# Loading q and k in runs of eight rows, sorting them on VectorE and turning all of them by DMA

## The chip, the core and the metric

The kernel runs on one core of one Trainium2 chip. The core has four compute engines with one instruction queue each: TensorE (PE in the profile) multiplies matrices and writes to PSUM, VectorE (DVE) and ScalarE (ACT) work element by element, and GpSimd (POOL) does simple element work and issues the DMAs that convert float32 to bfloat16. SyncE (SP) computes nothing; its queue issues the remaining DMAs, the transposing ones among them. Each engine takes its own instructions strictly in order, and an instruction that waits for a semaphore holds back everything behind it on the same engine.

The metric is the time of one execution on the device in microseconds. Before the change it is 306.56 us (median of 3 runs, 305.95 to 306.98).

## The reference

Sliding-window causal attention is followed by a two-matrix network with an x·cos(x) gate. Shapes: q, k and v are (8 batches, 8 heads, 576 positions, 64), `w_in` is 512 x 2048, `w_out` 2048 x 512, and the output 4608 x 512 in float32.

```python
window = 64
scores = (q @ k.transpose(0, 1, 3, 2)) / sqrt(64)
rel = pos[:, None] - pos[None, :]
scores = where((rel >= 0) & (rel < window), scores, -1e9)
attn = softmax(scores)
x = (attn @ v).transpose(0, 2, 1, 3).reshape(4608, 512)
h = x @ w_in
out = (h * cos(h)) @ w_out
```

## The kernel before

**Tiles of tokens.** The 4608 rows of x are nine tiles of 512 tokens. Tile 0 is handled by steps written out by hand (the string `FIRST`). Tiles 1 to 8 go through the loop over `mt`; one turn of it is called a stage here. A stage has two halves. In the first, TensorE makes sixteen products `h_ps` (L458, four matmuls each), ScalarE takes a sine of each (L597), and VectorE multiplies the two into `gT` (L600); these sixteen multiplications are called gates 0 to 15. In the second half TensorE makes four products `out_ps` (L611), each of which sums over all sixteen slices of `gT` in order. The sixteen `h_ps` take turns in five PSUM banks, so TensorE can be at most five products ahead of the gates.

**Attention.** In stage b-1 the scores of batch b are computed in two bursts (`burst_scores`, matmuls at L289), one just after the first half of the stage and one in the second half. They go in nine groups per batch: VectorE masks and takes the maximum (`g_max`, L326), ScalarE takes exponentials (`g_exp`, L338), GpSimd normalizes into `w` (`g_norm`, L355), and SP turns `w` into `wT` by a transposing DMA (`g_trans`, L374). At the end of the stage `values` (L390) multiplies `wT` with v, and `put_x` copies the result to `xT`, the input of the next stage. Of batch b's nine groups the next stage's tile needs only the first ones: four at stage 1's end (besides two that go through TensorE), five at stage 2's, four at stage 3's and 4's, two at stage 5's.

**q and k.** The scores need q and k with the head dimension on the partitions, so both must be turned. For batches 0 and 1 this is done on TensorE. For batches 2 to 7, `load_chunk` (L166) loads each of q and k in six chunks of 96 positions, all eight heads at once: rows of 64 numbers, issued by GpSimd, converted to bfloat16 on the way. Chunks of k are turned by DMA (`turn_k`, L239, six per batch). Of q, `TURNED` gives the number of chunks that DMA turns (`turn_q`, L227): none for batches 2 and 3, two for 4, 5 and 6, and six for 7. The remaining chunks are turned by TensorE (`transposed`, L203, into the PSUM tile `tq_ps`) and copied to SBUF by VectorE (`put_q`, a COPY at L121).

**The order.** Nothing is scheduled automatically. `at(time, function, ...)` puts steps on a list, and `pump(time)` issues those that are due; 32 units of that time make a stage, gate `ff` is followed by `pump(base + ff)`, and the second half covers units 16 to 32. The order of the steps in this list is the order on every engine's queue, SP's and GpSimd's among them. `t0 - T` in the code is the start of stage b-2, `t0` that of stage b-1.

Of the kernel before, what the change touches and what calls it, by code (L numbers as in the profile page):

```python
# [10 lines left out]
def _safe_warn(msg, *a, **kw):  # L11
# [13 lines left out]
NC, NP = 6, 96  # L25
# [5 lines left out]
RC = 9  # L31
# [8 lines left out]
TURNED = {4: 2, 5: 2, 6: 2, 7: 6}  # L40
# [26 lines left out]
def kernel(  # L67
# [28 lines left out]
    qsets = [const.tile([128, PAIRS, S], BF16, name=f"qT{i}") for i in range(2)]  # L96
    vtiles = [const.tile([128, NU - 1, d_model], BF16, name=f"v{i}") for i in range(2)]
# [44 lines left out]
    def rows_tile(name):  # L142
        return ld.tile([128, NC * H * D], BF16, tag=name, name=name)

    def load_heads(name, b, p0=0, n=PAIRS):
        if (name, b) not in st:
            st[name, b] = rows_tile(name)[:, 0:PAIRS * RC * D].rearrange("p (a x) -> p a x", a=PAIRS)
        src = {"q": q, "k": k}[name][b, 2 * p0:2 * p0 + 2 * n]
        nc.gpsimd.dma_start(out=st[name, b][:, p0:p0 + n],  # L149
                            in_=src.rearrange("(a h) (p c) d -> (h p) a (c d)", h=2, c=RC))  # L150
# [6 lines left out]
    def cast_plain(name, engine):  # L157
        if (name, 0) not in st:
            st[name, 0] = rows_tile(name)[:, 0:PAIRS * RC * D].rearrange("p (a x) -> p a x", a=PAIRS)
        copy(engine, st[name, 0][:, 0], st.pop(("rows", name)))  # L160

    def load_chunk(name, b, c):
        if (name, b) not in st:
            st[name, b] = rows_tile(name)[0:NP].rearrange("p (c x) -> p c x", c=NC)
        src = {"q": q, "k": k}[name][b, :, c * NP:c * NP + NP]
        nc.gpsimd.dma_start(out=st[name, b][:, c].rearrange("p (h d) -> p h d", h=H),  # L166
                            in_=src.rearrange("h p d -> p h d"))
# [25 lines left out]
    def transposed(name, b, p):  # L193
        t_ps = ps_t.tile([128, S], BF16, tag="t", name=f"t{name}_ps")
        of = st[name, b]
        if b < 2:
            for c in range(RC):
                for h in range(2):
                    d = slice(64 * h, 64 * h + 64)
                    nc.tensor.transpose(t_ps[d, 64 * c:64 * c + 64], of[d, p, 64 * c:64 * c + 64], ident[d, d])  # L200
        else:
            for c in range(TURNED.get(b, 0) if name == "q" else 0, NC):
                nc.tensor.transpose(t_ps[:, NP * c:NP * c + NP], of[:, c, 128 * p:128 * p + 128], ident[:NP, :NP])  # L203
# [3 lines left out]
    def in_order(t_ps, to, b):  # L207
        return (t_ps.rearrange("d (c p) -> d p c", c=RC), to.rearrange("d (p c) -> d p c", c=RC)) if b < 2 else (t_ps, to)
# [4 lines left out]
    def put_q(b, p, engine=None):  # L213
        if b > 1:
            lo = TURNED.get(b, 0) * NP
            copy(engine, qsets[b % 2][:, p, lo:], st.pop(("tq", b, p))[:, lo:])
            return
        of, to = in_order(st.pop(("tq", b, p)), qsets[b][:, p], b)
# [7 lines left out]
    def turn_q(b, c):  # L226
        nc.sync.dma_start(out=qsets[b % 2][:, :, c * NP:c * NP + NP], in_=st["q", b][:, c], transpose=True)  # L227
# [4 lines left out]
    def k_tile(b):  # L232
        if ("kA", b) not in st:
            st["kA", b] = ka = att.tile([128, PAIRS, S], BF16, tag="kT", name="kT", bufs=2)
# [3 lines left out]
    def turn_k(b, c):  # L238
        nc.sync.dma_start(out=k_tile(b)[:, :, c * NP:c * NP + NP], in_=st["k", b][:, c], transpose=True)  # L239

    def put_k(b, p, engine="a"):
        kt = k_tile(b)[:, p]
# [408 lines left out]
```

## Time and profile before

| | |
|---|---|
| time, median of 3 runs | 306.56 us (305.95 to 306.98) |
| span of the profiled execution, first to last instruction | 304.8 us |
| median less this span | 1.8 us |
| PE busy | 293.2 us, 96% of the span |
| DVE busy | 217.4 us, 71% |
| ACT busy | 233.7 us, 77% |
| POOL busy | 195.8 us, 64% |
| share of PE in the chain of waits that ended last | 90% |
| DMA packets on GpSimd's queue (q0) | 100192, 18.06 MB |
| DMA packets on SP's queue (q1) | 57808, 22.66 MB |

The profile describes one execution, and its own time is the span and what lies before the first and after the last instruction. A row of the grouped view gives the line of the code, the engine, the operation, output and inputs by their names in the program, the shape, the count, then busy time in all and the mean duration of one in nanoseconds. A row of the timeline gives start and duration in microseconds, engine, line and what was done; "x6" means that six such instructions are merged into the row. A row of the chain of waits has only start, duration, and engine with line. SPq is the queue of SP: its rows are the time that issuing takes, not the transfer; "to landing" is from the start of the issue until the data has arrived.

### The profile page before, as it was taken

The page shows a single profiled execution, that of the slowest core. Times are in us where ns is not written, and L with a number is a line of the kernel's source. Part 1 is how long each engine was busy: PE and PEld are TensorE (multiplying, and loading weights), DVE is VectorE, ACT ScalarE, POOL GpSimd, SP SyncE. Part 2 cuts the span into 40 slices and gives each one's busy share as a digit, 9 for nine tenths or more (in the row PEclk, how much of TensorE's full clock was granted, in tenths as well). Part 3 has the DMA queues.
Part 4 walks back from the last instruction along what each step waited for, and adds up shares of the span by engine and source line. Part 5 has one row for each costly group of instructions (what it writes and reads, how often), then busy time and mean ns, then how long its engine had stood idle before and what let it go on. Part 6 is the DMA issues. An engine that isn't in the chain of part 4 may idle for free.

```text
span 304.8 us, 8261 instructions
## 1 busy us (share of the span) xinstructions
PE 293.2 (96%) x2840; PEld 154.4 (51%) x2840; DVE 217.4 (71%) x868; ACT 233.7 (77%) x783; POOL 195.8 (64%) x226
## 2 busy tenths in 40 slices
PE   3789999999999999999999999999999999999995
PEld 3667854644455445444544444444544454454443
DVE  3797888898888877787678867886778677236701
ACT  5998699878986799779976998699869986116500
POOL 8899568986999579985998599769804930000000
PEclk9999999999999999999999999999999999999999
DMA  7999999999979995999999999999996852011011
GB/s 144 175 203 184 196 189 142 103 132 169 232 115 115 228 147 80 106 153 233 133 116 150 223 138 109 128 235 148 107 123 147 139 120 98 0 71 69 3 69 69
DMA packets 158186, 41.44 MB, mean 136 GB/s; under 512 B 146944, under 2 KB 153408, under 8 KB 158144
## 3 DMA queue, kind: packets, MB, share of 16 engines
q0 software_dynamic: 100192, 18.06, 80.8%
q1 hardware_dynamic: 57808, 22.66, 40.7%
q8 instruction: 22, 0.36, 0.5%
q14 instruction: 20, 0.16, 0.2%
q10 hardware_dynamic: 144, 0.20, 0.2%
HBM read 36.70 MB, written 9.44 MB: 151 GB/s over the span
## 4 chain that ended last, share of the span: by engine, by line
PE 90%; DVE 3%; DMA 2%; POOL 2%; ACT 1%; issue 1%; POOLq 0%
PE h_ps L458 37%; PE out_ps L611 36%; PE out_ps L441 5%; PE h_ps L422 4%; PE s_ps L289 3%; PE o_ps L390 3%; DMA k<-in_k_dram 2%; PE tq_ps L203 1%; PE out_ps L470 1%; DVE negm L321 1%; POOL q L149 1%; PE s_ps L311 1%; POOL k L149 1%; ACT e L338 0%; DVE wT L121 0%
## 5 line engine op out<-in xcount | busy, mean ns | idle before, releaser
L458 PE MATMUL h_ps<-xT,w_in 128*128 128x512 bf16 x512 | 115.1, 379 | 0.2
L611 PE MATMUL out_ps<-w_out,gT 128*128 128x512 bf16 x496 | 110.0, 379 | 0.0
L600 DVE TENSOR_TENSOR gT<-h_ps,sin 128x512 bf16<-128x512 f32 x128 | 85.1, 688 | 29.3 <-ACT sin L597 28.7
L338 ACT ACTIVATE e<-s,negm 128x128 f32<-128x128 f32 (+1 forms) x256 | 97.2, 382 | 1.7 <-POOL v L121 1.0
L597 ACT ACTIVATE sin<-h_ps 128x512 f32<-128x512 f32 x128 | 73.8, 598 | 31.4 <-PE h_ps L458 30.8
L355 POOL TENSOR_TENSOR w<-e,rden 128x512 bf16<-128x512 f32 (+1 forms) x68 | 69.3, 1033 | 30.8 <-DVE rden L348 25.0
L458 PEld LDWEIGHTS <-w_in 128*128 128x128 bf16 x512 | 48.9, 98 | 54.7
L611 PEld LDWEIGHTS <-gT 128*128 128x128 bf16 x496 | 47.4, 98 | 56.1
L326 DVE CUSTOM_DVE_ANT_0 s<-s_ps,mask 128x128 f32<-128x128 f32 (+1 forms) x256 | 56.1, 277 | 1.7 <-PE s_ps L311 1.4
L338 ACT ACTIVATION_READ_ACCUMULATOR e<-s,negm 128x1 f32 x256 | 48.3, 189 | 0.0
L172 POOL DMA_DIRECT2D v<-in_v_dram x40 | 34.1, 870 | 1.0 <-DMA q<-in_q_dram 1.0
L166 POOL DMA_DIRECT2D q<-in_q_dram x36 | 28.7, 797 | 7.6 <-DMA v<-in_v_dram 2.5
L166 POOL DMA_DIRECT2D k<-in_k_dram x36 | 28.5, 792 | 6.4 <-DMA k<-in_k_dram 4.5
L121 ACT COPY out_sb<-out_ps 128x512 f32<-128x512 f32 (+1 forms) x16 | 9.0, 563 | 23.9 <-PE out_ps L611 18.4
L348 DVE RECIPROCAL rden<-den 128x4 f32<-128x4 f32 (+1 forms) x73 | 12.2, 167 | 19.4 <-ACT e L338 19.0
L121 POOL COPY v<-v 64x1536 bf16<-64x1536 bf16 (+3 forms) x16 | 22.9, 1433 | 0.4
L121 DVE COPY out_sb<-out_ps 128x512 f32<-128x512 f32 x20 | 13.7, 687 | 12.1 <-PE out_ps L611 12.0
L121 DVE CAST xT<-o_ps 128x512 bf16<-128x512 f32 x24 | 15.6, 679 | 8.6 <-PE o_ps L390 8.4
L326 DVE DVE_READ_ACCUMULATOR2_ANT negm<- 128x1 f32 x256 | 21.3, 83 | 0.1
L441 PE MATMUL out_ps<-w_out,gT 128*128 128x512 bf16 x64 | 14.8, 380 | 0.0
L422 PE MATMUL h_ps<-xT,w_in 128*128 128x256 bf16 x128 | 14.6, 273 | 0.0
L422 PEld LDWEIGHTS <-w_in 128*128 128x128 bf16 x128 | 12.3, 98 | 1.4
(67 smaller groups left out, 230.9 us busy)
## 6 DMA issues: line engine op xcount, KB each, us to landing
out_dram<-out_sb SPq DMA_DIRECT2D x16, 512.0 KB, 7.3
v<-in_v_dram POOLq DMA_DIRECT2D x32, 128.0 KB, 6.0
q<-in_q_dram POOLq DMA_DIRECT2D x36, 96.0 KB, 8.7
k<-in_k_dram POOLq DMA_DIRECT2D x36, 96.0 KB, 8.6
w_in<-in_moe_w_in_dram POOLq DMA_DIRECT2D x4, 512.0 KB, 9.2
w_out<-in_moe_w_out_dram POOLq DMA_DIRECT2D x4, 512.0 KB, 11.0
q<-in_q_dram POOLq DMA_DIRECT2D x7, 144.0 KB, 6.5
k<-in_k_dram POOLq DMA_DIRECT2D x7, 144.0 KB, 6.7
```

What stands on the lines that cost most here:

```text
L121: {"a": nc.scalar.copy, "p": nc.gpsimd.tensor_copy}.get(engine, nc.vector.tensor_copy)(out, in_)
L166: nc.gpsimd.dma_start(out=st[name, b][:, c].rearrange("p (h d) -> p h d", h=H), in_=src.rearrange("h p d -> p h d"))
L172: nc.gpsimd.dma_start(out=vt.rearrange("p (h d) -> p h d", h=H), in_=v[b, :, c * 128:c * 128 + n, :].rearrange("h p d -> p h d"))
L326: nc.vector.tensor_tensor_reduce(out=s[:, u, c], in0=s_ps[:, u, c], in1=mask[:, 2 - j % 2 if j else 0, c], scale=-scale if b else -1.0, sc ...
L338: nc.scalar.activation(e[:, u, c], s[:, u, c], AF.Exp, bias=negm[:, u:u + 1], scale=1.0 if n < n_first else -1.0, accum_out=den[:, u:u + 1])
L355: (nc.gpsimd if engine == "p" else nc.vector).tensor_tensor(out=w[:, 0:u], in0=e[:, 0:u], op=ALU.mult, in1=rden[:, 0:u].unsqueeze(2).to_br ...
L422: nc.tensor.matmul(out=h_ps[:, half * e:half * e + half], lhsT=w_in_sb[:, ks, ff * 128:ff * 128 + 128], rhs=st["xT", 0][:, ks, half * g:ha ...
L441: nc.tensor.matmul(out=st["out", m], lhsT=st["g", ff // 2][:, ff % 2, m * 128:m * 128 + 128], rhs=w_out_sb[:, ff], start=ff == 0, stop=ff ...
L458: nc.tensor.matmul(out=st["h", ff], lhsT=w_in_sb[:, ks, ff * 128:ff * 128 + 128], rhs=st["xT", mt][:, ks], start=start, stop=stop)
L597: nc.scalar.activation(sin, h_ps, AF.Sin, bias=math.pi / 2.0)
L600: nc.vector.tensor_tensor(out=gt[:, e], in0=h_ps, in1=sin, op=ALU.mult)
L611: nc.tensor.matmul(out=o_ps[e], lhsT=gT[ff // 2][:, ff % 2, ms * 128:ms * 128 + 128], rhs=w_out_sb[:, ff], start=ff == 0, stop=ff == n_ff - 1)
```

## The change

For batches 2 to 7 q and k are loaded in another shape. Position 8p+r of a head (r from 0 to 7) goes to partition p: 72 partitions, each with runs of eight rows, which lie together in DRAM. Four heads make one load, so q and k have two loads each per batch (`load_runs`). VectorE then copies each load into the one buffer `sorted_rows`, where r is outermost and the eight heads stand side by side (`sort_runs`, four copies of 72 x 2048 per batch). [...] q lands in a tile `q_turned` of which there is one, and GpSimd brings it into the order of positions (`put_runs`, four copies of 128 x 576 per batch). k stays as it lands, the eight slices 80 apart; the score matmuls read it with that stride and write their results to PSUM with a stride of eight numbers. `TURNED`, the TensorE transposes of q for batches 2 to 6 and VectorE's copies of them are gone.

```diff
+    sorted_rows = const.tile([NP, RUN, d_model], BF16, name="sorted_rows")
...
-    def load_chunk(name, b, c):
...
+    def load_runs(name, b, part):
+        n = H // 2
+        st[name, b, part] = rows = rows_tile(name)[0:S // RUN, 0:n * RUN * D].rearrange("p (h x) -> p h x", h=n)
+        src = {"q": q, "k": k}[name][b, n * part:n * part + n]
+        nc.gpsimd.dma_start(out=rows, in_=src.rearrange("h (p r) d -> p h (r d)", r=RUN))
+
+    def sort_runs(name, b, part):
+        n = H // 2
+        to = sorted_rows[0:S // RUN, :, n * D * part:n * D * part + n * D]
+        nc.vector.tensor_copy(to.rearrange("p r (h d) -> p r h d", h=n),
+                              st.pop((name, b, part)).rearrange("p h (r d) -> p r h d", r=RUN))
...
-    def turn_q(b, c):
-        nc.sync.dma_start(out=qsets[b % 2][:, :, c * NP:c * NP + NP], in_=st["q", b][:, c], transpose=True)
+    def turn(name, b, c):
+        if name == "k":
+            to = k_tile(b)
+        else:
+            if c == 0:
+                st["q", b] = att.tile([128, PAIRS, RUN * NP], BF16, tag="q_turned", name="q_turned", bufs=1)
+            to = st["q", b]
+        nc.sync.dma_start(out=to[:, :, c * NP:c * NP + NP], in_=sorted_rows[:, c], transpose=True)
+
+    def put_runs(b, p):
+        of = st["q", b][:, p].rearrange("d (r x) -> d r x", r=RUN)[:, :, 0:S // RUN]
+        nc.gpsimd.tensor_copy(qsets[b % 2][:, p].rearrange("d (x r) -> d x r", r=RUN), of.rearrange("d r x -> d x r"))
...
-    def turn_k(b, c):
-        nc.sync.dma_start(out=k_tile(b)[:, :, c * NP:c * NP + NP], in_=st["k", b][:, c], transpose=True)
...
+        if b > 1:
+            rhs = st["kT", b, p].rearrange("d (r x) -> d r x", r=RUN)[:, :, lo // RUN:lo // RUN + 64 // RUN * chunks]
+            rhs = rhs.rearrange("d r (a t) -> d a r t", a=chunks)
+            return rhs[:, ::-1] if j and j % 2 == 0 else rhs, chunks
...
-                        nc.tensor.matmul(out=to.rearrange("p (a t) -> p a t", a=chunks),
+                        nc.tensor.matmul(out=to.rearrange("p (a t r) -> p a r t", a=chunks, r=RUN),
...
+        for part in range(2):
+            for i, name in enumerate("kq"):
+                if b > 2:
+                    at(t0 - T + (0.6, 0.7, 0.8, 0.9)[2 * i + part], load_runs, name, b, part)
+                at(t0 + (6, 6.6, 0.9, 1.5)[2 * i + part] if b == 2 else t0 - T + (9, 10.2, 12.6, 13.6)[2 * i + part], sort_runs, name, b, part)
+        for c in range(RUN):
+            at(t0 + 6.8 + 0.01 * c if b == 2 else t0 - T + 10.3 + 0.01 * c, turn, "k", b, c)
+            at(t0 + 1.6 + 0.01 * c if b == 2 else t0 - T + 13.7 + 0.01 * c, turn, "q", b, c)
+        for p in range(PAIRS):
+            at(t0 + (7.5 if b == 2 else 3.3) + p, put_runs, b, p)
         for c in range(5):
-            at(t0 + (8 if TURNED.get(b) == NC else 0.5) + c, load_v, b, c)
+            at(t0 + 7.6 + c, load_v, b, c)
...
+    nc.gpsimd.memset(sorted_rows[64:NP], 0.0)
```

For batches 3 to 7 the queues get these steps in stage b-2. VectorE: gate 9, first sort of k, gates 10 and 11, second sort of k, gates 12 and 13, first sort of q, gate 14, second sort of q, gate 15. SP: the eight turns of k, the eight turns of q, and behind them the `wT` transposes of that stage. Batch 2 has its own sorts and turns in stage 1, ahead of those of batch 3: q after gates 1 and 2, k after gates 6 and 7.

More of the change, by code (lines that the diff above doesn't have):

```diff
@@ L24 @@
 NU = 9
-NC, NP = 6, 96
+RUN, NP = 8, 80
 GF = 4
@@ L39 @@
 FILL = (6, 12)
-TURNED = {4: 2, 5: 2, 6: 2, 7: 6}
 FIRST = (
@@ L158, in cast_plain @@
         if (name, 0) not in st:
-            st[name, 0] = rows_tile(name)[:, 0:PAIRS * RC * D].rearrange("p (a x) -> p a x", a=PAIRS)
+            st[name, 0] = rows_tile(name).rearrange("p (a x) -> p a x", a=PAIRS)
         copy(engine, st[name, 0][:, 0], st.pop(("rows", name)))
-    def load_chunk(name, b, c):
[L163 to L167, printed above, removed]
+    def load_runs(name, b, part):
[8 more added lines that the diff above has]
+                              st.pop((name, b, part)).rearrange("p h (r d) -> p r h d", r=RUN))
     def load_v(b, c):
@@ L195, in transposed, with in_order @@
         of = st[name, b]
[L196 to L203, printed above, removed]
-        return t_ps
-    def in_order(t_ps, to, b):
-        return (t_ps.rearrange("d (c p) -> d p c", c=RC), to.rearrange("d (p c) -> d p c", c=RC)) if b < 2 else (t_ps, to)
+        for c in range(RC):
+            for h in range(2):
+                d = slice(64 * h, 64 * h + 64)
+                nc.tensor.transpose(t_ps[d, 64 * c:64 * c + 64], of[d, p, 64 * c:64 * c + 64], ident[d, d])
+        return t_ps
+    def in_order(t_ps, to):
+        return t_ps.rearrange("d (c p) -> d p c", c=RC), to.rearrange("d (p c) -> d p c", c=RC)
     def tr_q(b, p):
@@ L213, in put_q @@
     def put_q(b, p, engine=None):
[L214 to L218, printed above, removed]
+        of, to = in_order(st.pop(("tq", b, p)), qsets[b][:, p])
         if b:
```

23 lines of the change are left out of this document (5 added, 18 removed), and 8 rows, old and new, of the table FIRST.

## The prediction

> **What bounds the kernel now.** I read the page first, then the chain of waits, then the timelines of VectorE and SP. In the page:
>
> ```profile
> span 304.8 us, 8261 instructions
> PE 293.2 (96%) x2840; PEld 154.4 (51%) x2840; DVE 217.4 (71%) x868; ACT 233.7 (77%) x783; POOL 195.8 (64%) x226
> PE 90%; DVE 3%; DMA 2%; POOL 2%; ACT 1%; issue 1%; POOLq 0%
> ```
>
> TensorE is busy for 96% of the span and makes 90% of the chain that ended last: it sets the time, and an edit to it saves its full length as long as no other queue becomes late. The chain shows where the stages begin:
>
> ```profile
> 57.53 2.59 PE h_ps L458 x12
> 60.12 0.26 PE tq_ps L203 x6
> ...
> 89.33 2.75 PE h_ps L458 x12
> ...
> 120.83 2.75 PE h_ps L458 x12
> 123.58 0.17 PE tq_ps L203 x4
> ...
> 152.00 2.75 PE h_ps L458 x12
> ...
> 183.21 2.75 PE h_ps L458 x12
> ...
> 213.23 1.13 PE o_ps L390 x64
> 214.36 0.03 issue
> 214.38 13.97 PE h_ps L458 x64
> 228.36 0.52 PE s_ps L289 x32
> ```
>
> Stages 1 to 5 start at 57.53, 89.33, 120.83, 152.00 and 183.21 and last 31.80, 31.50, 31.17, 31.21 and 31.17 us. From the values to the next stage it is 1.15 us (213.23 to 214.38). The transposes of q that the change removes are on the chain: six in 0.26 us, four in 0.17, so 96 of them (8 x 6 + 12 x 4) make 8 x 0.26 + 12 x 0.17 = 4.1 us. That is all the change can save on TensorE.
>
> **What the added turns cost.** These are the queue of SP and the landing times:
>
> ```profile
> L239 SPq DMA_TRANSPOSE kT<-k x36: 1182/1216/2490, 59.3 to 228.2; - x36
> L374 SPq DMA_TRANSPOSE wT<-w x60: 1188/1209/2997, 43.3 to 248.3; - x60
> 59.28 8.77 SPq L239 DMA_TRANSPOSE kT<-k  x6
> 223.03 5.08 SPq L227 DMA_TRANSPOSE qT<-q  x4
> 196.49 1.08 SPq L478 DMA_DIRECT2D out_dram<-out_sb  x2
> kT<-k SPq DMA_TRANSPOSE x36, 5.0
> qT<-q SPq DMA_TRANSPOSE x12, 2.4
> ```
>
> Issuing one transpose holds SP for at least 1.18 us, and the median is the same for slices of 96 rows (kT, 1216 ns) and of 128 (wT, 1209 ns): the size does not matter, so I give a slice of 80 rows the same. In a row they go 1.27 us apart where little else moves (5.08/4) and 1.46 apart beside many small loads (8.77/6). I take 1.27, as the change removes the small loads, and 2.4 us from an issue to its landing (bounds 2.3 and 5.0). Eight turns thus take 7 x 1.27 + 2.4 = 11.3 us until the last has landed, and free SP after 8 x 1.27 = 10.2 us.
>
> All sorts write the one buffer `sorted_rows`, and the turns read it. So the first sort of q must wait until the eight turns of k have landed. In the built kernel's instruction list it waits for all eight semaphores of SP's DMAs. Behind it in VectorE's queue stand gate 14, the second sort of q, gate 15 and the batch's maxima, and TensorE waits for gate 14 at the fifteenth matmul of the second half.
>
> The gates' times are those of stage 6, which has no transposes, and of stage 1:
>
> ```profile
> 217.37 3.71 DVE L600 TENSOR_TENSOR gT<-h_ps,sin 128x512 bf16<-128x512 f32 x6 [1.78 <-ACT sin L597]
> 223.84 0.69 DVE L600 TENSOR_TENSOR gT<-h_ps,sin 128x512 bf16<-128x512 f32 x1 [0.17 <-ACT sin L597]
> 229.03 0.69 DVE L600 TENSOR_TENSOR gT<-h_ps,sin 128x512 bf16<-128x512 f32 x1 [0.17 <-ACT sin L597]
> 60.86 2.48 DVE L600 TENSOR_TENSOR gT<-h_ps,sin 128x512 bf16<-128x512 f32 x4 [1.00 <-ACT sin L597]
> 50.28 1.12 DVE L121 COPY v<-v 64x2048 bf16<-64x2048 bf16 x1
> 50.80 1.07 POOL L121 COPY v<-v 64x512 bf16<-64x512 bf16 x1
> 19.30 0.29 DVE L121 COPY v<-v 64x512 bf16<-64x512 bf16 x1
> 236.80 1.04 POOL L355 TENSOR_TENSOR w<-e,rden 128x512 bf16<-128x512 f32 x1 [0.55 <-POOL w L355]
> ```
>
> Gate 9 (223.84) ends 10.15 us after the stage's start, gate 15 (229.03) 15.3 us after it; back to back a gate takes 0.62 (3.71/6, 2.48/4). A sort of 72 x 2048 bf16 isn't in the trace. The one copy of that width took 1.12 us while GpSimd was copying too; a quarter of it took 0.29 us, four of which make 1.17 with the fixed part counted four times. I take 0.9, with bounds 0.29 and 1.17.
>
> **One stage, from its start** (stages 2 to 5): first sort of k ends 10.15 + 0.9 = 11.05, gates 10 and 11 at 12.3, second sort of k 13.2. The turns of k have landed at 13.2 + 11.3 = 24.5. First sort of q 25.4, gate 14 at 26.0, second sort 26.9, gate 15 at 27.5, or 12.2 us later than now. The turns of q hold SP from 26.9 to 37.1. Only then come the `wT` transposes. In stage 6 the fourth `w` is ready 8.1 us after gate 15 (237.84 less 229.72), here at 35.6, so it doesn't wait for them; the n-th `wT` lands at 37.1 + 1.27(n-1) + 2.4, and 1.15 later the next stage starts:
>
> - stage 2 needs five: 45.7 against 31.50, so 14.2 more
> - stages 3 and 4 need four: 44.5 against 31.17 and 31.21, so 13.3 more each
> - stage 5 needs two: 41.9 against 31.17, so 10.7 more
>
> TensorE's own path is shorter: after gate 15 at 27.5 it has three products of 3.46 us (13.97/64 x 16) and the scores left, some 40 us with the values.
>
> **Stage 1** has the chain twice. Gate 1 ends at 4.6 (60.86 + 1.24 less 57.53). Sort of q 5.5, gate 2 at 6.1, second sort 7.0; turns of q landed 18.3; sort of k 19.2, gate 7 at 19.8, second sort 20.7; turns of k landed 32.0; first sort of batch 3's k 32.9, gates 10 and 11, second sort 35.0; landed 46.3; sort of q 47.2, gate 14, second sort 48.7; turns of q issued by 58.9; the fourth `wT` landed 65.1, next stage at 66.3. Against 31.80 that is 34.5 more.
>
> **Start.** GpSimd's clearing of 16 x 4096 stands ahead of its first loads, and these are on the chain:
>
> ```profile
> 0.31 0.10 POOL L635 MEMSET const-bfloat16-1.0<- 128x1 bf16 x1
> 0.74 0.20 POOL masks.py:197 MEMSET ident<- 128x128 bf16 x1 [0.29 <-POOLq L635]
> 5.38 0.49 POOL q L149
> 5.87 6.71 DMA k<-in_k_dram
> ```
>
> 127 more elements cost about 0.1 us, so 4096 cost 3.4 us (0 if it takes no longer than the small one). Everything behind the loads moves by that much.
>
> **The rest lies beside this work.** The loads shrink on GpSimd:
>
> ```profile
> L166 POOL DMA_DIRECT2D q<-in_q_dram x36 | 28.7, 797 | 7.6 <-DMA v<-in_v_dram 2.5
> q<-in_q_dram POOLq DMA_DIRECT2D x7, 144.0 KB, 6.5
> L121 DVE COPY qT<-tq_ps 128x576 bf16<-128x576 bf16 x12 | 6.4, 544 | 0.0
> ```
>
> Twelve issues of 0.8 us per batch become four; a load of 144 KB lands in 6.5 us, before the sort at 10.15. Without that cover a stage would lose what the load is late. Putting q in order (24 copies, about 1.0 us each by the 64 x 512 copy) fits where GpSimd waits for VectorE, well ahead of the scores; were it not, each batch would pay up to 4 us. VectorE loses the copies of `tq_ps` (6.4 us, and less for the 384-wide ones), which were never on the chain.
>
> The scores' strided reads and writes are in no row. 32 matmuls take 0.52 us now; I take no change (a gain has no reason, a loss could be several times that), because in stages 1 to 5 TensorE will be waiting anyway, and only stage 6 could show it. [...]
>
> **Sum.** 34.5 + 14.2 + 13.3 + 13.3 + 10.7 + 3.4 = 89.4 on a span of 304.8; the 4.1 us of transposes are already out of the new stages. That gives 394.2, and with the 1.8 us by which the median exceeds the span, 396 us.
>
> **Rivals.**
> - *Turns cost their bytes only* (not slower). If eight turns landed within about 4 us (second sort of k at 13.2, TensorE reaching gate 14 at 17.5), VectorE would never hold TensorE up: 304.8 - 4.1 + 1.8 = 302.5, or 305.9 if the clearing is paid. Against it: no transpose of 108 was issued in under 1.18 us. 3%.
> [...]
> - *Only SP's queue binds*, the sort's wait being met earlier than I think. SP then has 25 transposes and two stores per stage, 25 x 1.27 + 1.1 = 32.9 us against 31.2; in stage 1 it has 41, 53.2 us. 21.4 + 4 x 1.6 + 3.4 more: 338 us. 7%.
> - *Crowded turns*: steps of 1.46 and landings nearer 5 us, as for kT before. 103 steps and 12 landings lie on the path (stage 1: 32 and 4; then 19, 18, 18, 16 and two each): 103 x 0.19 + 12 x 2.6 = 51 us more, 447 us. For it: GpSimd still loads v at units 8 to 12, beside the first turns of k. Against: the other turns come when nothing is loaded. 10%.
>
> **How the numbers follow.** My forecast has 80%: 396 us, alone 372 to 430 (steps at 1.18 take 9 us off, the 24 sorts at 0.29 take 15 off; at 1.17 they add 6, steps at 1.46 add 20, half of the crowded landings 16). Reaching toward the rivals, 368 to 440. About 0.3% is what a measurement of this kernel can tell from no change. The first rival is the only case that isn't slower: faster 2%, within 0.3% 1%, slower 97%.
>
> **What would show it.** Right: VectorE's first sort of q stands behind a wait of some 11 us on SP's DMAs in each of stages 1 to 5, TensorE idles before the fifteenth matmul of the second half and before the values, the eight turns take about 10 us of SP, and stages 2 to 5 last 42 to 46 us, stage 1 about 66. Wrong: turns of 80 rows issued in well under 1.18 us, sorts of q that start at once, or stages 1 to 5 of some 31 us. Score matmuls of several times 16 ns, or a clearing under 1 us, would spoil single terms.

## The result and the profile after

The changed kernel takes 418.69 us (median of 5 runs, 415.57 to 419.53); the kernel before, on the same chip, 306.93 us (305.95 to 307.66). The ratio is 1.3621, with a 95% interval of 1.3572 to 1.3669. 396 us was predicted, with 368 to 440 as the range. The profiled execution has a span of 413.7 us, and the sum of the prediction, 394.2 us, is to be held against that.

From the page of the kernel after:

```profile
span 413.7 us, 8067 instructions
PE 315.6 (76%) x2712; PEld 161.8 (39%) x2744; DVE 223.8 (54%) x872; ACT 234.6 (57%) x783; POOL 192.1 (46%) x203
PE 42%; SPq 13%; issue 10%; ACT 9%; POOL 9%; DMA 8%; DVE 7%; DVEq 0%; POOLq 0%; ACTq 0%
```

TensorE's share of the chain that ended last falls from 90% to 42%, and SP's queue, which had none, stands in it with 13%. TensorE has fewer instructions and yet is busy for 22.4 us more (315.6 less 293.2). The products `h_ps` and `out_ps` take 396 and 401 ns per matmul, where it was 379, in stages 1 to 5 whose granted clock is 0.76 to 0.88 (the table of stretches below; 1.00 in the kernel before), and the score matmuls at L296 take 16.2 us in all, where it was 8.7. From the waits of the kernel after (total, times, longest):

```profile
DVE sorted_rows L171 <- DMA kT<-sorted_rows: 55.4, 5, 12.1
PE out_ps L617 <- DVE gT L606: 44.0, 10, 9.5
PE h_ps L465 <- DVE gT L606: 26.1, 3, 16.3
DVE sorted_rows L171 <- DMA v<-in_v_dram: 17.6, 1, 17.6
PE o_ps L397 <- DMA wT<-w: 10.3, 11, 1.4
```

Five times, once in each of stages 1 to 5, VectorE's first sort of q waits some 11 us until the turns of k have landed; TensorE then waits for the gates behind that sort, and at the stage's end for `wT`. In stage 2 the sine for gate 14 is ready at 149.20; the gate runs at 161.66, behind the sort, which starts at 161.05 after a wait of 11.72 us. The wait of 17.6 us, put down to a load of v, is batch 3's first sort of k in stage 1: the chain names the last turn of batch 2's k there (`91.98 7.29 DMA kT<-sorted_rows` below). SP's timeline (batch 2's turns in stage 1, then stage 2 from 148.21):

```profile
66.46 10.96 SPq L230 DMA_TRANSPOSE q_turned<-sorted_rows  x8
80.99 12.25 SPq L230 DMA_TRANSPOSE kT<-sorted_rows  x8
...
148.21 11.58 SPq L230 DMA_TRANSPOSE kT<-sorted_rows  x8
163.01 11.16 SPq L230 DMA_TRANSPOSE q_turned<-sorted_rows  x8
174.28 12.88 SPq L381 DMA_TRANSPOSE wT<-w  x9
```

A merged row runs from the first issue to the end of the last, and includes time in which SP waits for the next `w`. The first `wT` of stage 2 did not wait for one: the fourth `w` is ready at 171.16, and the first `wT` is issued at 174.28, right behind the turns of q:

```profile
170.12 1.04 POOL L362 TENSOR_TENSOR w<-e,rden 128x512 bf16<-128x512 f32 x1 [0.50 <-DVE rden L355]
```

Busy times by stretch, one for each stage (start:end, length, busy time of each engine with its count, granted clock of TensorE, DMA share, GB/s):

```profile
60.00:134.81 74.81, 38.77 (x270) 17.82 (x271) 30.66 (x124) 27.60 (x100) 23.62 (x24) 0.76 0.68 91
134.81:183.48 48.67, 35.02 (x265) 16.68 (x265) 24.64 (x111) 27.28 (x95) 24.84 (x24) 0.85 0.71 106
183.48:231.10 47.62, 35.78 (x264) 16.89 (x265) 24.52 (x111) 27.59 (x95) 25.00 (x24) 0.86 0.79 110
231.10:278.09 46.99, 36.46 (x264) 17.04 (x265) 24.76 (x111) 27.42 (x95) 24.67 (x24) 0.85 0.81 114
278.09:322.20 44.11, 33.58 (x260) 15.78 (x265) 24.81 (x111) 27.29 (x95) 24.80 (x24) 0.88 0.94 116
322.20:353.72 31.52, 31.14 (x260) 15.38 (x264) 22.88 (x107) 27.33 (x95) 21.68 (x20) 1.00 0.74 104
```

Every stage that has turns is long, and stage 6, which has none, lasts 31.52 us against 30.52 before. Beside them stand the prediction's 66.3, 45.7, 44.5, 44.5 and 41.9 us for stages 1 to 5.

### The profile page after: what moved, and what is told of

Read it like the earlier page. It is cut to its first block, busy times and chain, and to the rows that moved or that the text cites. A ratio compares the mean times of both kernels' runs of the same rounds, so it can differ in the third digit from the quotient of the medians.

```text
span 413.7 us, 8067 instructions
## 1 busy us (share of the span) xinstructions
PE 315.6 (76%) x2712; PEld 161.8 (39%) x2744; DVE 223.8 (54%) x872; ACT 234.6 (57%) x783; POOL 192.1 (46%) x203
## 4 chain that ended last, share of the span: by engine, by line
PE 42%; SPq 13%; issue 10%; ACT 9%; POOL 9%; DMA 8%; DVE 7%; DVEq 0%; POOLq 0%; ACTq 0%
PE h_ps L465 20%; SPq L230 13%; PE out_ps L617 9%; ACT e L345 8%; DMA kT<-sorted_rows 4%; PE h_ps L429 3%; DMA wT<-w 3%; POOL w L362 3%; POOL v L121 3%; PE out_ps L448 3%; DVE gT L606 2%; PE o_ps L397 2%; DVE sorted_rows L171 2%; DVE s L333 1%; POOL v L177 1%
## 5 line engine op out<-in xcount | busy, mean ns | idle before, releaser
L617 PE MATMUL out_ps<-w_out,gT 128*128 128x512 bf16 x482 | 118.6, 401 | 45.4 <-DVE gT L606 44.0
L465 PE MATMUL h_ps<-xT,w_in 128*128 128x512 bf16 x498 | 118.6, 396 | 27.4 <-DVE gT L606 26.1
L606 DVE TENSOR_TENSOR gT<-h_ps,sin 128x512 bf16<-128x512 f32 x128 | 83.7, 685 | 30.9 <-ACT sin L603 30.9
L617 PEld LDWEIGHTS <-gT 128*128 128x128 bf16 x496 | 48.8, 102 | 110.1 <-DVE gT L606 48.9
L465 PEld LDWEIGHTS <-w_in 128*128 128x128 bf16 x512 | 51.5, 101 | 91.4 <-issue 36.5
L171 DVE COPY sorted_rows<-q 72x2048 bf16<-72x2048 bf16 x12 | 8.2, 684 | 55.4 <-DMA kT<-sorted_rows 55.4
L234 POOL COPY qT<-q_turned 128x576 bf16<-128x576 bf16 x24 | 30.3, 1319 | 0.0
L171 DVE COPY sorted_rows<-k 72x2048 bf16<-72x2048 bf16 x12 | 9.1, 759 | 27.8 <-DMA v<-in_v_dram 17.6
L397 PE MATMUL o_ps<-wT,v 128*64 128x64 bf16 x512 | 13.8, 211 | 10.5 <-DMA wT<-w 10.3
L121 DVE COPY out_sb<-out_ps 128x512 f32<-128x512 f32 x20 | 13.7, 687 | 12.4 <-PE out_ps L617 12.2
L166 POOL DMA_DIRECT2D k<-in_k_dram x12 | 9.5, 796 | 22.5 <-DVE sorted_rows L171 22.4
## 6 DMA issues: line engine op xcount, KB each, us to landing
w_out<-in_moe_w_out_dram POOLq DMA_DIRECT2D x4, 512.0 KB, 10.8
```

What stands on the lines that cost most here:

```text
L121: {"a": nc.scalar.copy, "p": nc.gpsimd.tensor_copy}.get(engine, nc.vector.tensor_copy)(out, in_)
L171: nc.vector.tensor_copy(to.rearrange("p r (h d) -> p r h d", h=n), st.pop((name, b, part)).rearrange("p h (r d) -> p r h d", r=RUN))
L234: nc.gpsimd.tensor_copy(qsets[b % 2][:, p].rearrange("d (x r) -> d x r", r=RUN), of.rearrange("d r x -> d x r"))
L465: nc.tensor.matmul(out=st["h", ff], lhsT=w_in_sb[:, ks, ff * 128:ff * 128 + 128], rhs=st["xT", mt][:, ks], start=start, stop=stop)
L606: nc.vector.tensor_tensor(out=gt[:, e], in0=h_ps, in1=sin, op=ALU.mult)
L617: nc.tensor.matmul(out=o_ps[e], lhsT=gT[ff // 2][:, ff % 2, ms * 128:ms * 128 + 128], rhs=w_out_sb[:, ff], start=ff == 0, stop=ff == n_ff - 1)
```

## The experiments

Each was timed against the kernel before (305.8 to 306.8 us by group), in 4 runs unless another number is named.

**1. Two buffers.** q and k are sorted into buffers of their own; `gT` loses two of its ten buffers to make room.

```diff
-    sorted_rows = const.tile([NP, RUN, d_model], BF16, name="sorted_rows")
+    sorted_of = {name: const.tile([NP, RUN, d_model], BF16, name=f"sorted_{name}") for name in "qk"}
```

> q and k are sorted into two buffers instead of one, so the first sort of q needn't wait for the turns of k; to make room there are 8 tiles of gT instead of 10, which should cost nothing. Theory (two queues in series: the wait in VectorE, and the wT transposes behind sixteen turns on SP): the gates run through and TensorE's wait for gate 14 goes, but wT still comes late. From a stage's start the second sort of k ends at 12.6 (10.15, two sorts of 0.6, two gates), sixteen turns of 1.28 hold SP until 33.1, the n-th wT lands 1.28(n-1) + 2.4 later and the next stage starts 1.15 after it: 41.8 for stage 2, 40.5 for stages 3 and 4, 37.9 for stage 5, about 62 for stage 1. Against 74.1, 48.7, 47.6, 46.9 and 44.1 that is 39 less, a span of about 375. Rival (the wait in VectorE is the whole price): stages of about 31, a span near 310. Rival (SP's order alone is the price): no change, about 414.

One run: 401.32 us, span 399.5. Its waits, and SP in stage 2, which starts at 129.83:

```profile
PE o_ps L397 <- DMA wT<-w: 46.0, 19, 7.9
DVE sorted_k L171 <- DMA kT<-sorted_k: 22.5, 1, 22.5
```

```profile
144.04 12.48 SPq L230 DMA_TRANSPOSE kT<-sorted_k  x8
156.65 10.24 SPq L230 DMA_TRANSPOSE q_turned<-sorted_q  x8
166.99 12.97 SPq L381 DMA_TRANSPOSE wT<-w  x9
```

The sorts of q no longer wait for the turns of k; one sort still waits 22.5 us, in stage 1, where batch 3's k must wait until batch 2's has been turned. The span falls by only 14 us. Stages 1 to 5 are 19 us shorter together; 3.5 us are lost at the start, where GpSimd now clears two buffers (stage 1 begins at 63.38), and 1.7 in stage 6. TensorE now waits 46.0 us for `wT`: the first `wT` is issued 37.2 us after the stage's start (166.99 less 129.83), and was at 39.5 (174.28 less 134.81). With one buffer the turns of q follow those of k by some 3 us; with two they follow at once. Most of the wait for the buffer lay beside the time that SP needs for k anyway.

**2. Merged turns.** One buffer, but k is turned by four DMAs of two slices and q by one of eight.

```diff
-        nc.sync.dma_start(out=to[:, :, c * NP:c * NP + NP], in_=sorted_rows[:, c], transpose=True)
+        n = TURN[name]
+        nc.sync.dma_start(out=to[:, PAIRS * c:PAIRS * (c + n)],
+                          in_=sorted_rows[:, c:c + n].rearrange("p r x -> p (r x)"), transpose=True)
```

> The changed kernel with one buffer, but a transposing DMA turns two slices of k at once (four issues per batch) and all eight of q (one issue). Theory (an issue costs about 1.2 us whatever its size, as 96 and 128 rows cost the same): turns of k have landed 3 x 1.27 + 2.4 after the second sort, so q is sorted from 18.8 to 20.7, its turn leaves SP at 22, and the fourth wT waits for w (8.1 after gate 15, so 29.4): stages 2 to 5 of about 33, stage 1 of about 42, a span of about 326. Rival (the issue costs by the number of blocks of 128 columns, which was four in each transpose before): 2.5 us for two slices and 10 for eight, the span as it is, about 414.

One run: 382.59 us, span 380.8. SP's issues (minimum, median, maximum in ns) and the landings:

```profile
L232 SPq DMA_TRANSPOSE kT<-sorted_rows x24: 1203/1349/3207, 75.4 to 263.7; - x24
L232 SPq DMA_TRANSPOSE q_turned<-sorted_rows x6: 3263/3377/3392, 66.1 to 273.5; - x6
```

```profile
kT<-sorted_rows SPq DMA_TRANSPOSE x24, 7.6
q_turned<-sorted_rows SPq DMA_TRANSPOSE x6, 5.9
```

Neither a fixed price nor one by bytes. Issuing two slices takes hardly longer than one (1.35 for 1.25 us), eight take 3.38, but the median landing goes from 2.4 to 5.9 us for q and from 4.2 to 7.6 for k. About half of the queue's time for the turns is saved, the first sort of q still waits, and the span falls by 33 us (413.7 less 380.8), not by the 88 that the theory called for.

**3. The strided PSUM writes alone.** The kernel before, with the scores' columns written to PSUM with the changed kernel's stride. The columns then stand in another order, so its output isn't the reference's.

```diff
-                        nc.tensor.matmul(out=to.rearrange("p (a t) -> p a t", a=chunks),
+                        nc.tensor.matmul(out=to.rearrange("p (a t r) -> p a r t", a=chunks, r=8),
```

> The kernel before, whose score matmuls of batches 2 to 7 write to PSUM with a stride of eight numbers, as in the changed kernel, but read k without strides; the columns of the scores come out in another order, so this output isn't the reference's. Theory (the stride of the writes is what makes 32 score matmuls take 0.89 us instead of 0.52, and 40 take 1.43 instead of 0.79 in stage 6 of the changed kernel): 1.0 us more in each of six stages, all on TensorE's path, a time of 313 against 307. Rival (the strided read of k is the cause): no change.

Two runs: 312.75 us (312.35 and 313.14), ratio 1.0217 (1.0174 to 1.0259). The score matmuls before, and in this run:

```profile
L289 PE MATMUL s_ps<-kT,qT 64*64 64x128 bf16 x384 | 8.2, 218 | 0.0
```

```profile
L289 PE MATMUL s_ps<-kT,qT 64*64 64x128 bf16 x384 | 14.1, 308 | 0.0
```

A matmul takes 308 ns for 218, and the kernel that TensorE bounds is 6 us slower: each of stages 1 to 6 lasts 1.0 us longer.

**4. The clearing later.** The buffer `sorted_rows` has 80 partitions, of which the rows fill 72; each turn takes all 80, and GpSimd sets the last 16 to zero once. Here it does so behind most of tile 0's work, not ahead of its first loads.

```diff
-    nc.gpsimd.memset(sorted_rows[64:NP], 0.0)
...
+             "z": lambda: nc.gpsimd.memset(sorted_rows[64:NP], 0.0), "io": put_steps,
```

> The changed kernel with the clearing of the 16 spare partitions issued later on GpSimd, behind the first load of batch 2's q instead of ahead of the first loads of all. Theory (the clearing delays everything by its 3.5 us): stage 1 starts about 3.2 us earlier, at 57.5 instead of 60.8, and the span falls to about 410.5. Rival (the start has slack): stage 1 starts where it does.

One run: 415.18 us, span 413.4. The clearing runs from 39.97 us. In TensorE's timeline the values now wait for `wT`:

```profile
57.05 0.66 PE L397 MATMUL o_ps<-wT,v 128*64 128x64 bf16 x30 [1.80 <-DMA wT<-w]
```

Tile 0 runs 3 us earlier at first. Then the clearing stands ahead of five `w` in GpSimd's queue, and stage 1 begins at 59.23 us, 0.6 earlier than with the clearing at the start (59.87; 57.36 in the kernel before). Most of the price is paid in either place, as far as one run tells.

**5. The turns of q behind `wT`.** Two buffers as in the first; SP gets k's turns, the nine `wT`, then q's turns, and GpSimd puts q in order correspondingly later.

```diff
-            at(t0 + 1.6 + 0.01 * c if b == 2 else t0 - T + 13.7 + 0.01 * c, turn, "q", b, c)
+            at(t0 + 1.6 + 0.01 * c if b == 2 else t0 - 0.7 + 0.01 * c, turn, "q", b, c)
```

> Two buffers as in the run of two buffers (401 us), and for batches 3 to 7 the eight turns of q are issued behind the last wT transpose of the stage instead of ahead of the first; GpSimd puts q in order correspondingly later in the next stage. If that run was slow because sixteen turns stand ahead of wT in SP's queue, wT now waits for eight turns only: k's turns end 23 to 25 us after the stage's start, the fourth wT lands some 8 us later, and stages 2 to 5 last 35 to 37 us instead of 42 to 47: 355 to 370 us, with stage 1 still long. If SP's total of 25 transposes is what counts, wherever they stand, the stages stay at 25 x 1.35 + 1.1 = 35 us as the least, so this end can't be told from the first; but if VectorE's sorts or TensorE's clock were what holds it, the time stays at 395 to 405.

415.51 us (413.71 to 416.93). The expectation failed, and the time lies in none of the ranges that it names. What waits now:

```profile
POOL qT L234 <- DMA q_turned<-sorted_q: 76.2, 6, 14.9
```

The last turn of q lands only when the first scores are due, GpSimd must still put it in order, and TensorE's scores wait for that (59.9 us in all). Moving the turns behind `wT` doesn't free the path, it puts them ahead of the scores. The run does not tell the queue's order from its total.

**6. The loads of v early.** They go back to where the kernel before had them.

```diff
-            at(t0 + 7.6 + c, load_v, b, c)
+            at(t0 + (7.6 if b == 2 else 0.5) + c, load_v, b, c)
```

> The changed kernel with the loads of v of batches 3 to 7 back at the place they had before (units 0.5 to 4.5 of the stage, not 7.6 to 11.6), so that they are not under way when the turns of k are issued. If these loads are what makes the last turn of k land after 4.2 us (q's after 2.4) and the eight issues take 11.6 us, landing falls to about 2.5 and the issues to about 10.3: the sort of q is released 2 to 3 us earlier in each of stages 2 to 5, 405 to 411 us in all. If k's turns are slow for another reason (where they are written, or the loads of q and k), the time stays within 3 us of 418.7.

419.01 us (418.06 to 421.04): no gain. k's turns do land sooner, at a median of 3.6 us where it was 4.2, but the loads of v are now ahead of those of k, which land after a median of 7.6 us (6.7 before), and the sort waits for these instead:

```profile
246.67 0.69 DVE L171 COPY sorted_rows<-k 72x2048 bf16<-72x2048 bf16 x1 [1.97 <-DMA k<-in_k_dram]
```

**7 and 8. Everything early, then PSUM in order.** Two buffers, merged turns, q and k loaded a stage earlier and sorted in the first half of the stage, the clearing on VectorE. The eighth also writes the scores without a stride and lets VectorE's masking maximum read them with one.

```diff
+                    at(t0 - T + (0.6, 0.7, 0.8, 0.9)[2 * i + part] if b == 3 else t0 - 2 * T + (18 if b == 4 else 16.6) + 0.1 * i + 0.2 * part, load_runs, name, b, part)
+                at(t0 + (2, 2.6, 0.9, 1.5)[2 * i + part] if b == 2 else t0 - T + (15.2, 17, 10, 11.2)[2 * i + part] if b == 3
+                   else t0 - T + (1, 2.2, 8, 9.2)[2 * i + part], sort_runs, name, b, part)
...
-                        nc.tensor.matmul(out=to.rearrange("p (a t r) -> p a r t", a=chunks, r=RUN),
+                        nc.tensor.matmul(out=to.rearrange("p (r a t) -> p r a t", a=chunks, r=RUN),
...
+                    of = of.rearrange("p (r x) -> p x r", r=RUN)
```

> All waits that the runs so far blame are moved at once: two sorted buffers, q turned by one DMA and k by four, q and k loaded a stage earlier so that k is sorted after gates 1 and 2 and q after gates 8 and 9 (batches 4 to 7; batch 3 in stage 1 with q ahead of k), and the spare partitions cleared by VectorE, which is idle then. SP has 5 issues of some 9 us in all per stage in place of 16 of 22, nothing in VectorE's queue stands behind a turn, and wT starts free. If the account is complete, each of stages 1 to 6 lasts the 31.2 us of before, less 0.6 without TensorE's transposes of q (stages 1 to 5), plus 1.0 for the scores' stride: 304.8 - 4.1 + 6.0 + 1.8 = 308.5 us, and up to 316 if stage 1 still waits; TensorE's granted clock is at 1.0 in stages 2 to 6. If merged transposes crowd out wT's (9 took 15 to 18 us beside them), the values wait: 325 to 345. Within 5 us of the kernel before or not is what it tells.

> As the run before it, and the score matmuls read k in the same slices but write PSUM without a stride (the columns stand in the order r, position); VectorE's masking maximum reads PSUM with the stride instead. If the stride of the writes is the whole cost of the scores (5.6 us in the kernel before with strided writes), it is 5 to 6 us faster than that run: 303 us if that one is at 308.5. If the read stride of k costs as much, or VectorE's 256 instructions slow down (276 ns each), no gain.

351.67 us (345.68 to 359.08) and 350.43 us (345.37 to 354.72); the fastest of each, 345.68 and 345.37, differ by 0.1%. The gain over the change is some 68 us by the medians, and not the 110 that the account called for. SP in the eighth, stages 2 and 5 (which start at 112.77 and 225.80):

```profile
121.12 5.74 SPq L232 DMA_TRANSPOSE kT<-sorted_k  x4
126.97 14.03 SPq L232 DMA_TRANSPOSE q_turned<-sorted_q  x1
141.10 12.50 SPq L388 DMA_TRANSPOSE wT<-w  x9
...
240.71 4.67 SPq L232 DMA_TRANSPOSE q_turned<-sorted_q  x1
```

In stages 2 to 4 (37.7, 37.4 and 38.0 us long) one DMA for q holds SP for 13 to 14 us; in stage 5, in which GpSimd loads no q or k, for 4.67, and that stage lasts 31.85. The score matmuls are back at 223 ns (320 in the seventh, 218 in the kernel before), so the stride of the writes was nearly their whole loss here, and reading k in slices cost 5 ns at the most:

```profile
L299 PE MATMUL s_ps<-kT,qT 64*64 64x128 bf16 x384 | 8.6, 223 | 0.0
```

The 5 us expected from it don't show in the time: the runs scatter by 13 and 9 us, and TensorE waits in stages 1 to 4 anyway. Stage 6, which has no turns, does show its share: 30.51 us, where the seventh has 31.52.

**9. The loads apart from the turns.** As the eighth, with the loads of q and k at units 20 to 24.5 of the stage before and those of v from unit 14.

```diff
-            at(t0 + 7.6 + c, load_v, b, c)
+            at(t0 + (7.6 if b == 2 else 14) + 0.8 * c, load_v, b, c)
```

> The run with PSUM written in order (350 us; its stages 2 to 4 last 37.4 to 38 us, its stage 5, in which no q or k is loaded, 31.4) with the loads of q and k moved from 10 to 14 us after a stage's start, where they meet the turns, to units 20 to 24.5 of the stage before, v's loads from unit 7.6 to 14, the sorts of k by two gates and of q by one later, and VectorE's clearing behind the start. If the single turn of q holds SP for 13 to 16 us only because these loads share the DMA engines with it, it takes 3.4 to 5 us again, wT is not held back, and stages 2 to 4 last 31.5 to 33.5 us: 327 to 335 us, the rest being stage 1 (51 us) and the start. If a turn behind four turns of k waits for those whatever else moves, stages 2 to 4 stay near 37.5 and the time at 345 to 352. The loads now lie beside wT's transposes; if that costs as much, the time stays too, but with q's turn short and wT's long.

345.75 us (336.88 to 353.15; the profiled execution took 347.08). q's turn in stage 2, which starts at 121.37, and the time from issue to landing (minimum, median, maximum) of the four `wT` issued from 141 to 147 us:

```profile
135.87 3.55 SPq L232 DMA_TRANSPOSE q_turned<-sorted_q  x1
```

```profile
DMA to landing us min/median/max: 2.4/7.0/7.3
```

q's turn holds SP for 3.55 us here, and 3.24 to 3.97 in stages 2 to 5, where it was 13 to 14 us beside the loads in stages 2 to 4 of the eighth. Now the loads of k and q, issued from 142.8 us on, meet `wT`, which lands after 7.0 us; the nine of stage 2 of the eighth have a median of 2.5. Stages 2 to 4 of this execution last 34.6, 31.8 and 35.3 us, shorter than the eighth's, and stage 1 lasts 61.7, where it was 52.8. Beside loads from DRAM the transposes took longer in these runs (q's turn 14.03 us for 3.55, the landing of `wT` 7.0 for 2.5), and in both places to which the loads were moved (experiments 8 and 9) they met some; what the two share isn't shown. No version with everything on DMA came near the kernel before.

**10. k's half alone.** k as the change has it, q loaded and turned as before.

```diff
+            at(t_q, tr_q, b, p)
+            at(t_q + 0.02, put_q, b, p)
...
+            at(t0 + (1, 1.6)[part] if b == 2 else t0 - T + (9, 10.2)[part], sort_runs, "k", b, part)
```

> Half of the change alone: k in runs, sorted and turned as the change has it (eight turns, one buffer, strided scores, clearing on GpSimd), q loaded in chunks and turned as before (TensorE and the two or six turns by DMA). The buffer now has one user per stage, so no sort waits for a turn except batch 3's in stage 1 (batch 2's turns before it have 10 us by then). My account: TensorE's 304.8, scores 5 to 6 more, start 2.5 more, and the first wT behind k's turns: they end 23.4 us after the stage's start, the fourth or fifth wT lands 6 to 9 us later, at 29.5 to 32, so each of stages 2 to 5 is held by 0 to 2 us: 314 to 324 us. If turning k in eight is itself what costs (crowded landings, SP's queue), it is nearer to half of the whole loss: 350 to 365. If it takes 395 or more, q's half had little to do with it.

338.69 us (336.9 to 340.32), ratio 1.1061 (1.1011 to 1.111). Stages 2 to 5 last 35.8, 34.6, 32.3 and 33.7 us, where the account allowed some 34 at most; stage 1 lasts 47.9, and there the expectation failed. In this run k's turns land after a median of 6.9 us, and batch 2's had not landed when batch 3's k was to be sorted (the profile puts the wait down to a `wT` issued right behind them):

```profile
85.48 0.69 DVE L180 COPY sorted_rows<-k 72x2048 bf16<-72x2048 bf16 x1 [13.15 <-DMA wT<-w]
```

Of the 112 us, some 33 are there with k's half alone; the other 79 appear only with q's half beside it.

**11. Matmuls in the wait.** 28 matmuls into the PSUM bank of the next product, ahead of the product that waits for gate 14.

```diff
+                    if e == ms0 == 0 and ff == n_ff - 2 and mt < 6:
+                        for _ in range(28):
+                            nc.tensor.matmul(out=o_ps[1], lhsT=gT[0][:, 0, 0:128], rhs=w_out_sb[:, 0], start=True, stop=True)
```

> The changed kernel with 28 matmuls of 128x512 put into the wait of TensorE for gate 14 in stages 1 to 5 (some 9 us of idle; they take 6 to 7.5 and write a PSUM bank that the next product clears). If the granted clock falls because TensorE idles (0.50 in the wait, 0.73 to 0.88 after it), and that is where some 12 us beyond my sum come from, the clock after the wait is higher and stages 2 to 5 get 0.5 to 2 us shorter each: 408 to 415 us against 418.7. If the clock is set by something else, or what follows is held by the turns and not by TensorE, no change within 2 us; if the fillers overrun the wait, slower by what they overrun.

422.21 us (421.33 to 423.54). The matmuls turned out to wait for a gate behind the same sort, so they ran after the wait and not in it; in stage 2:

```profile
163.64 7.87 PE L619 MATMUL out_ps<-w_out,gT 128*128 128x512 bf16 x28 [8.16 <-DVE gT L606]
```

They don't fill the wait that they were made for. They lengthen TensorE's work behind it instead, up to the end of the stage: it no longer waits for `wT` at all (10.3 us in the changed kernel), and stages 2 to 5 last 47.5, 48.0, 47.5 and 47.5 us, where it was 48.7, 47.6, 47.0 and 44.1; stage 1 is 2.4 us longer. Counted from the end of gate 14 in both kernels, TensorE without the 7.87 us had an estimated 5 to 8 us to spare in stages 2 to 4, and some 3 in stage 5, whose next tile needs only two `wT`.

They also show something of the clock. TensorE is busy for 7.9 to 8.0 of the 8 us before each of stages 2 to 5, and each of them opens at a granted clock of 1.00; in the changed kernel it is busy for 4.4 us before stage 3, and that stage opens at 0.62. The first 5 us of stage 3, in the changed kernel and in this one:

```profile
183.48:188.48 5.00, 4.78 (x17) 1.93 (x16) 0.92 (x4) 2.62 (x4) 4.72 (x6) 0.62 0.68 92
```

```profile
184.99:189.99 5.00, 4.94 (x23) 2.26 (x24) 3.22 (x7) 4.38 (x7) 4.29 (x6) 1.00 0.91 72
```

At 0.62 the stage's first matmuls take 634 ns, at 1.00 they take 379. The first turn of k is issued 12.9 us after the start in each of stages 2 to 5 here (in stage 3 at 197.90); in the changed kernel's stage 3 it was 14.5.

**12. No loads beside the turns.** Batches 4 to 7 sort batch 3's rows again, and v is not loaded from batch 3 on, so the output isn't the reference's.

```diff
+        if b > 3:
+            st[name, b, part] = st["kept", name, part]
+            return
```

> The changed kernel without the loads of q and k for batches 4 to 7 and of v for batches 3 to 7: the sorts read batch 3's loads again and everything else runs as before, so stages 2 to 5 have turns, wT and stores and no load from DRAM beside them (part of the input is not read). If the loads are what makes the steps longer than the 1.27 us that I took (k's eight 10.3 to 11.6 us, q's 10.8 to 11.2, nine wT 12.2 to 14.5) and lets k land after 2.4 to 4 us, all steps fall to 1.27 to 1.30 and stages 2 to 5 come to the 45.7, 44.5, 44.5 and 41.9 us of my sum: 10.7 us less, 406 to 410 us. If the steps are long for SP's own sake or for the stores, or the granted clock holds the gates up, the time stays within 3 us of 418.7 and the steps at 1.35 to 1.55. In no case does it come near the kernel before, since the order of the turns is kept.

409.76 us (407.27 to 412.27), 8.9 less than the change; span of the profiled execution 409.3. Stages 2 to 5 last 48.4, 46.3, 44.4 and 42.7 us (by the stretches: 136.34, 184.74, 230.99, 275.37 and 318.06 are their bounds). k lands after a median of 2.4 us. SP in stage 4:

```profile
243.59 10.24 SPq L233 DMA_TRANSPOSE kT<-sorted_rows  x8
257.20 10.69 SPq L233 DMA_TRANSPOSE q_turned<-sorted_rows  x8
267.99 12.36 SPq L384 DMA_TRANSPOSE wT<-w  x9
```

k's steps fall to 1.28 us, as expected; q's (1.34) and `wT`'s (1.37) fall less. Stages 4 and 5 come within 0.1 and 0.8 us of the sum of the prediction, stages 2 and 3 stay 2.7 and 1.8 above it. In these two the first turn of k is 1.0 to 1.1 us late, and they open at a clock of 0.66 and 0.67 (first 5 us); stages 4 and 5 open at 1.00.

## Why the prediction was right, and where it was 23 us short

**The account of the span.** By its stages (measured less forecast, us): stage 1 starts at 59.87 and not at 57.53 + 3.4, -1.1; it lasts 74.9, +8.6; stages 2 to 5 +3.0, +3.1, +2.5 and +2.2; stage 6 +1.0; what follows +0.1. Unrounded that makes 19.5, and 394.2 + 19.5 = 413.7. The remaining 3 us are the profiled execution, which was the fastest of the five (415.57 us, the median 3.1 above).

**TensorE's gain of 4.1 us** cannot be seen: in stages 1 to 5 TensorE no longer sets the end.

**The price of a turn.** Right. 48 turns of q have a median of 1252 ns, those of k 1251, by the rows

```profile
L230 SPq DMA_TRANSPOSE q_turned<-sorted_rows x48: 1175/1252/2167, 66.5 to 316.0; - x48
L230 SPq DMA_TRANSPOSE kT<-sorted_rows x48: 1177/1251/2357, 81.0 to 300.2; - x48
L171 DVE COPY sorted_rows<-q x12: 678/679/690, 64.6 to 305.4; 72x2048 bf16<-72x2048 bf16 x12
```

but eight of them came 1.28 to 1.53 us apart, not 1.27 (10.24/8 to 12.25/8).

**The chain in a stage.** Right in its events and their order. After a stage's start came the first turn of k, the first of q, and the first `wT`:

| us after the start | forecast | stage 2 | 3 | 4 | 5 |
|---|---|---|---|---|---|
| first turn of k | 13.2 | 13.4 | 14.5 | 15.1 | 12.9 |
| first turn of q | 26.9 | 28.2 | 28.2 | 28.7 | 28.4 |
| first `wT` | 37.1 | 39.5 | 39.5 | 39.6 | 39.3 |
| next stage, forecast | | 45.7 | 44.5 | 44.5 | 41.9 |
| next stage, measured | | 48.7 | 47.6 | 47.0 | 44.1 |

From row to row the same figures give what each step of the chain took beyond the forecast (10.8 us in all):

| us over the forecast | stage 2 | 3 | 4 | 5 | sum | sum without loads (experiment 12) |
|---|---|---|---|---|---|---|
| start to first turn of k | 0.2 | 1.3 | 1.9 | -0.3 | 3.1 | 1.0 |
| to first turn of q | 1.1 | 0.0 | -0.1 | 1.8 | 2.8 | 0.0 |
| to first `wT` | 1.1 | 1.0 | 0.7 | 0.7 | 3.5 | 3.1 |
| to next stage | 0.6 | 0.8 | 0.0 | 0.0 | 1.4 | 1.1 |

The term that was too small is "I take 1.27, as the change removes the small loads, and 2.4 us from an issue to its landing", in two places. k's turns (second row) meet the loads that are left; without these loads (experiment 12) they take what was forecast. q's turns (third row) are 0.7 to 1.1 us too long in every stage, and nearly as much without the loads: one of the eight holds SP for 1.7 to 2.2 us. Why is not known.

The prediction has no term for the first row, which is the largest in stages 3 and 4. These stages open at a granted clock of 0.62 and 0.60 (first 5 us; 0.87 in stage 2, 1.00 in stage 5), their first gates come later, and so does the first sort of k. Experiments 11 and 12 agree: the four stages of 11 open at 1.00 and issue k 12.9 us after the start, and in 12 only the two stages that open low are late. TensorE is busy for 5.6, 4.4, 5.0 and 6.7 of the 8 us before stages 2 to 5; that its idling there is the reason for the low clock is a guess of the author's and isn't shown, as no run changes the idling alone.

**Stage 1.** Most of its 8.6 us comes from batch 2's turns of k. They were to have landed 32.0 us after the start; the last landed at 99.27, 39.4 after it. Of these 7.4 us, 0.4 is the first turn's start, 2.1 the steps between the eight (1.53 us each) and 4.9 the landing of the last, by this piece of the chain:

```profile
91.98 7.29 DMA kT<-sorted_rows
```

and GpSimd's timeline shows why the neighbours are there:

```profile
79.94 1.91 POOL L166 DMA_DIRECT2D k<-in_k_dram  x2 [22.43 <-DVE sorted_rows L171]
...
90.82 1.56 POOL L177 DMA_DIRECT2D v<-in_v_dram  x2
```

GpSimd waits 22.4 us for a sort to free the rows and then issues nine loads within 12.4 us, beside these very turns. The rival of crowded turns had this mechanism at 10%, with steps of 1.46 us and 2.6 us per landing; here it was 1.53 and 4.9, at one place.

**What held the stage.** The prediction has the wait for `sorted_rows` and SP's queue in one chain and doesn't say which of them counts for more. Experiment 1 tells: without the wait for the turns of k only 14 us come back (19 in stages 1 to 5), as SP would still be turning k, and TensorE waits for `wT`. Sixteen turns ahead of `wT` in one queue, begun 13 us into the stage, are the larger part. The rival "only SP's queue binds" had 338 us because it let SP work through the whole stage, whereas before the first sort, behind gate 9, SP has nothing of the next batch to turn.

**The scores.** The zero was taken for stages 1 to 5, and stage 6 alone was to show a loss; it lost 1.0 us. In experiment 3 a score matmul that writes PSUM with the stride took 308 ns for 218, 1.4 times, and each of stages 1 to 6 lasted 1.0 us longer.

**Turns at their bytes.** That rival falls: eight slices took 10.2 us and more, and merged into one DMA still 3.4 us of SP's queue and 5.9 to the landing (655 KB in 5.9 us are some 110 GB/s).

**The small terms.** A sort takes 0.68 us for q and 0.69 for k by the median, 1.16 at most (0.9 taken). The clearing takes 3.50 us (3.4 taken), of which 2.5 reach stage 1 (59.87 less 57.36). Putting q in order takes 1.32 us per copy, not 1.0, and nobody waits for it. The prediction took the 6.5 us of a load of 144 KB for the new loads, but these are twice as large:

```profile
q<-in_q_dram POOLq DMA_DIRECT2D x12, 288.0 KB, 11.2
k<-in_k_dram POOLq DMA_DIRECT2D x12, 288.0 KB, 6.7
```

In stages 2 to 5 they had landed before their sorts even so (the second load of k 11.7 us after the start at the latest, its sort from 12.1 us on).

## What to carry to other kernels

Saving work on the bounding engine by moving it to DMA pays only if the DMA's whole chain (rows ready, sort, issue, landing, and what the queue holds behind it) fits into the stage; here 4 us of TensorE were traded for a chain of 39 us in a stage of 31. Before giving a wait its full price, ask what the next queue in the chain would do without it: here the waits of 55.4 us for the buffer were worth 14 of the span (19 in stages 1 to 5, experiment 1), as most of them lay beside the time that SP needed for k anyway. And price a transfer beside its future neighbours, not by the median of a quiet stretch: k's turns were priced at 2.4 us to the landing and took a median of 4.2, and 2.4 without the loads (experiment 12).

## What had not been expected of the hardware

- One transposing DMA of eight slices held its queue for 3.3 to 3.4 us in experiment 2, where it is issued some 25 us after the stage's start (144.07 less 118.82 in stage 2) and the loads of q, issued at the start, land after a median of 11.4 us. It held it for 13 to 16 us in stages 2 to 4 of experiments 7 and 8, beside loads of q and k (in stage 2 of the eighth these are issued from 123.07 to 127.43 us, the turn at 126.97).
- Merging the issues shortened the queue's time (eight slices 3.4 us, not 10.2), but the landing of one DMA went from 2.4 to 5.9 us for q and, for k's pairs of slices, from 4.2 to 7.6.
- VectorE's read of PSUM with a stride of 16 numbers cost nothing measurable (a masked maximum takes 284 ns in experiment 8 as in 7, without the stride), while a score matmul with TensorE's write at a stride of eight numbers took 308 ns for 218 (experiment 3).
